# Attention output transposed by the DMA crossbar instead of TensorE and VectorE

## The chip, the cores and the metric

The kernel runs on one core of a Trainium2 chip. The metric is the device time of one execution in microseconds. Runs of one comparison share a chip and are taken in turn with the kernel before. A ratio is the mean time of one kernel's fast runs over the mean of the other's fast runs in the same rounds, so it is not quite the ratio of the medians quoted beside it. The experiments ran on several chips, each beside its own runs of the kernel before; the median of the kernel before moves from 243.7 to 244.9 us between these groups, so small differences between runs of different groups say nothing.

## The reference, cut to what matters

```python
B, H, S, D = 4, 8, 768, 64      # attention in chunks of 32, context 16 left, 8 right, 8 memory slots
out[:, :, c_start:c_end] = softmax(scale * q_c @ k_full.T) @ v_full      # for each chunk
x = attn_out.transpose(0, 2, 1, 3).reshape(B * S, H * D)                 # 3072 x 512
h = x @ w_in                                                             # 512 -> 2048
g = h + sin(alpha * h) ** 2 / (alpha + 1e-9)
return g @ w_out                                                         # 2048 -> 512
```

The first MLP matmul needs x with its 512 columns on the partitions. The attention gives it with the rows on the partitions, so each block of 96 rows has to be transposed.

## The kernel before

The kernel takes one batch after the other. While the attention of batch i+1 runs (a "burst"), the second MLP matmul of batch i is fed between its pieces, one matmul (`o`) at a time from a `Stream`. One block of a burst:

```python
def pv(b, j, pt):
    x_blk = blk.tile([QW, H, D], BF, name="x_blk")        # blk: 3 buffers
    ...
    for h in range(H):
        nc.tensor.matmul(otv[:, h // 4, h % 4, :], pt[...], vws[b % 2][:, h, j, 0:D + 1])
    nc.vector.reciprocal(rv, ...)
    nc.vector.tensor_tensor(out=x_blk..., in0=otv..., in1=rv..., op=ALU.mult)
    return x_blk, ot

def xt(xT, j, x_blk, ot):            # one block later
    ...
    for kt in range(KT):
        nc.tensor.transpose(xtp[:, kt, :], x_blk[:, 2 * kt:2 * kt + 2, :]..., ident[0:QW, 0:QW])
    nc.vector.tensor_copy(xT[:, :, QW * j:QW * j + QW], xtp)

def burst(b, stream, shares, lag):
    ...
        ptl[s] = qk_exp(s)                       # scores (sc) and exp
        stream.take(n // 3, True)
        xbl[s - lag] = pv(b, s - lag, ptl.pop(s - lag))
        stream.take((n + 1) // 3, True)
        xt(xT, s - lag - 1, *xbl.pop(s - lag - 1))
        stream.take((n + 2) // 3, True)
```

After the burst comes an MLP stage: 16 groups of the first MLP matmul (`hT`), of which each reads all of xT. The q, k and v of the batch after next are loaded by GpSimd's queue, issued around the start of a burst (`load_qk(i + 2)`, `load_v_all(i + 2)`). The output stores are issued by SyncE.

The softmax here doesn't subtract the row's maximum and nothing guards it: scores larger than these inputs give would overflow.

## Time and profile before

| | kernel before |
|---|---|
| time, median of three runs | 243.7 us |
| TensorE busy, clock | 91% of the span, 0.986 |
| burst 1, 2, 3 (first sc to last x_blk) | 16.9, 19.8, 20.0 us |
| end of the burst (last x_blk to the fifth matmul of the first hT group) | 2.8, 2.8, 2.5 us |

The busy shares tell which engine is fullest over the span, but a change in one stage has to be read from that stage. So the table has bursts and their ends, taken from start and end times in the timeline. The fifth matmul of the first hT group is where the second half of xT is needed in the new order, and is a fair mark in both.

### The profile page before, as it was taken

How to read it: one execution, taken by the hardware profiler on the slowest of the kernel's cores; microseconds unless marked ns; L12 is line 12 of the kernel's file. 1: busy time of each engine (PE TensorE's matmuls, PEld its weight loads, DVE VectorE, ACT ScalarE, POOL GpSimd, SP SyncE). 2: the span in 40 equal slices, each digit the busy share in tenths (PEclk: the TensorE clock that was granted, in tenths of full speed). 3: DMA queues.
4: the chain of work that ended last, by engine and by line, in shares of the span. 5: the costliest groups of instructions: out<-in, count | busy, mean ns of one | idle time of the engine just before them, and what ended most of it. 6: DMA issues, size and time to landing. Idle time of an engine off the chain costs nothing.

```text
span 243.4 us, 4498 instructions
## 1 busy us (share of the span) xinstructions
PE 222.6 (91%) x1785; PEld 123.0 (51%) x1785; DVE 160.2 (66%) x287; ACT 154.7 (64%) x237; POOL 73.3 (30%) x96
## 2 busy tenths in 40 slices
PE   6798899989989899898999997998999999899994
PEld 2355565545445455454455653554455555453453
DVE  3496969999268658969457775868657267876101
ACT  3489599973975467798464784678765675871000
POOL 8899865214712114157200222120000002020000
PEclk9799999999999999999999997999999999999999
DMA  6999999999999610109992101001111101101122
GB/s 75 165 130 83 161 194 204 207 198 134 190 208 134 74 46 0 44 4 181 154 151 66 46 0 43 0 3 43 46 43 47 43 0 46 43 0 40 46 89 86
DMA packets 53852, 21.11 MB, mean 87 GB/s; under 512 B 36296, under 2 KB 50888, under 8 KB 53832
## 3 DMA queue, kind: packets, MB, share of 16 engines
q0 software_dynamic: 47616, 14.40, 70.7%
q1 hardware_dynamic: 6216, 6.43, 8.9%
q8 instruction: 14, 0.23, 0.4%
q14 instruction: 6, 0.05, 0.1%
HBM read 28.91 MB, written 6.29 MB: 145 GB/s over the span
## 4 chain that ended last, share of the span: by engine, by line
PE 48%; DVE 20%; ACT 12%; issue 12%; POOL 3%; DMA 2%; POOLq 1%; DVEq 0%; ACTq 0%
PE o L393 26%; PE hT L341 10%; DVE gT L367 8%; DVE s L358 5%; ACT pt L275 4%; ACT u L353 4%; ACT s L356 3%; PE ot L288 3%; PE sc L266 3%; POOL s L358 2%; DMA q_bf<-in_q_dram 2%; DVE kTi L243 2%; PE ot L306 2%; PE o L382 1%; DVE x_blk L293 1%
## 5 line engine op out<-in xcount | busy, mean ns | idle before, releaser
L393 PE MATMUL o<-w_out_sb,gT 128*128 128x512 bf16 x368 | 99.0, 381 | 0.7 <-DVE gT L367 0.4
L341 PE MATMUL hT<-xT,w_in_sb 128*128 128x384 bf16 x488 | 88.8, 329 | 3.9 <-DVE gT L367 3.6
L367 DVE SCALAR_TENSOR_TENSOR gT<-s,inv_alpha,hT 128x768 bf16<-128x768 f32 x61 | 61.2, 1012 | 30.0 <-ACT s L356 21.6
L353 ACT ACTIVATE u<-hT,alpha_sb 128x768 f32<-128x768 f32 x61 | 54.7, 898 | 28.3 <-PE hT L341 27.1
L341 PEld LDWEIGHTS <-w_in_sb 128*128 128x128 bf16 x512 | 49.8, 99 | 39.7 <-issue 7.4
L275 ACT ACTIVATE pt<-sc,biasm 128x256 bf16<-128x256 f32 x96 | 37.6, 492 | 13.0 <-PE sc L266 13.0
L393 PEld LDWEIGHTS <-gT 128*128 128x128 bf16 x368 | 31.9, 98 | 26.9 <-DVE gT L367 1.4
L358 POOL TENSOR_TENSOR s<-u 128x768 f32<-128x768 f32 x6 | 8.8, 1465 | 73.7 <-ACT u L353 73.7
L356 ACT ACTIVATE s<-u 128x768 f32<-128x768 f32 x34 | 28.7, 843 | 1.1
L358 DVE TENSOR_TENSOR s<-u 128x768 f32<-128x768 f32 x24 | 24.7, 1029 | 0.9 <-ACT u L353 0.8
L226 POOL COPY pr<-q_bf 128x768 bf16<-128x768 bf16 x12 | 10.1, 838 | 43.7 <-PE tt_a L242 27.4
L293 DVE TENSOR_TENSOR x_blk<-ot,rinv 96x512 bf16<-96x512 f32 x32 | 22.0, 686 | 1.1
L292 DVE RECIPROCAL rinv<-ot 96x8 f32<-96x8 f32 x32 | 6.4, 201 | 20.1 <-PE ot L288 19.8
L402 ACT COPY o_sb<-o 128x512 f32<-128x512 f32 x11 | 6.4, 585 | 20.0 <-PE o L393 20.0
L400 DVE COPY o_sb<-o 128x512 f32<-128x512 f32 x12 | 8.2, 687 | 15.4 <-PE o L393 15.4
L288 PEld LDWEIGHTS <-pt 128*128 128x128 bf16 x256 | 11.9, 97 | 7.2 <-issue 2.3
L171 PE MATMUL z<-zeros 128*128 128x512 bf16 x37 | 13.9, 463 | 1.3 <-DVE zeros L165 1.3
L288 PE MATMUL ot<-vw,pt 128*128 128x65 bf16 x256 | 13.0, 193 | 0.8 <-ACT pt L275 0.6
L266 PEld LDWEIGHTS <-kTi 64*128 64x128 bf16 x256 | 6.9, 94 | 13.0 <-issue 6.6
L266 PE MATMUL sc<-qT,kTi 64*128 64x96 bf16 x256 | 11.4, 205 | 1.8 <-ACT pt L275 1.2
L257 PEld LDWEIGHTS <-pr 128*128 128x128 bf16 x96 | 6.6, 100 | 12.5 <-issue 8.0
L306 PEld LDWEIGHTS <-x_blk 96*128 96x128 bf16 x128 | 8.4, 97 | 6.6 <-DVE x_blk L293 1.6
(66 smaller groups left out, 182.1 us busy)
## 6 DMA issues: line engine op xcount, KB each, us to landing
out_dram<-o_sb SPq DMA_DIRECT2D x23, 256.0 KB, 2.1
k_bf<-in_k_dram POOLq DMA_DIRECT2D x3, 768.0 KB, 8.6
q_bf<-in_q_dram POOLq DMA_DIRECT2D x3, 768.0 KB, 12.6
vw<-in_v_dram POOLq DMA_DIRECT2D x6, 384.0 KB, 17.4
w_in_sb<-in_moe_w_in_dram POOLq DMA_DIRECT2D x8, 256.0 KB, 8.3
w_out_sb<-in_moe_w_out_dram POOLq DMA_DIRECT2D x4, 512.0 KB, 18.7
k_bf<-in_k_dram POOLq DMA_DIRECT2D x4, 192.0 KB, 6.2
q_bf<-in_q_dram POOLq DMA_DIRECT2D x4, 192.0 KB, 6.7
```

Source lines behind the costliest of these rows:

```text
L171: nc.tensor.matmul(z[:], zeros[:, 0:P], zeros[:])
L266: nc.tensor.matmul(sc[:, e, QW * hp:QW * hp + QW], kTi[64 * e:64 * e + 64, hp, 104 * j:104 * j + P], qT[64 * e:64 * e + 64, hp, QW * j:QW ...
L275: nc.scalar.activation(pt[:, 0:H * QW].rearrange("p (g e c) -> p e g c", g=4, e=2)[:, :, :, 32 * m:32 * m + 32], sc[:, :, 0:4 * QW].rearra ...
L288: nc.tensor.matmul(otv[:, h // 4, h % 4, :], pt[:, QW * h:QW * h + P], vws[b % 2][:, h, j, 0:D + 1])
L293: nc.vector.tensor_tensor(out=x_blk[:].rearrange("p (g e) d -> p g e d", g=2), in0=otv[0:QW, :, :, 0:D], in1=rv.unsqueeze(3).to_broadcast( ...
L306: nc.tensor.transpose(xtp[:, kt, :], x_blk[:, 2 * kt:2 * kt + 2, :].rearrange("p e d -> p (e d)"), ident[0:QW, 0:QW])
L341: nc.tensor.matmul(hts[hf][:, 0:HALF], w_in_sb[:, kt, P * ft:P * ft + P], xT[:, kt, HALF * hf:HALF * hf + HALF], start=(kt == 0), stop=(kt ...
L353: nc.scalar.activation(u[:], hT[:, :, 0:HALF], ACTF.Sin, scale=alpha_sb[:, ft:ft + 1])
L356: nc.scalar.activation(s2[:], u[:], ACTF.Square)
L358: (nc.vector if sq == "D" else nc.gpsimd).tensor_tensor(out=s2[:], in0=u[:], in1=u[:], op=ALU.mult)
L367: nc.vector.scalar_tensor_tensor(out=gv, in0=s2[:], scalar=inv_alpha[:, ft:ft + 1], in1=hT[:, :, 0:HALF], op0=ALU.mult, op1=ALU.add)
L393: nc.tensor.matmul(o[:], gT[:, ft, P * s:P * s + P], w_out_sb[:, ft, :], start=(ft == 0), stop=(ft == FT - 1),)
```

## The change

The intent is to free TensorE, which is full in the bursts, of 96 transposes, and VectorE of 24 copies. `dma_start_transpose` is a transfer that writes a block transposed; it is issued by SyncE. "Landing" below is the moment at which the trace shows a transfer completed; the time to landing is counted from its issue. Batch 0 keeps the old way. Some o matmuls are moved behind the last block to cover the latency of the last transpose, and the first hT group reads the first half of xT's columns first.

```diff
-    blk = ctx.enter_context(tc.tile_pool(name="blk", bufs=3))
+    blk = ctx.enter_context(tc.tile_pool(name="blk", bufs=4))
@@ xt
-        if ot is None:
-            xtp = smp.tile([P, KT, QW], BF, name="xtp", tag="sm")[:]
-        else:
-            xtp = ot[:].bitcast(BF)[:, 0, 640:640 + KT * QW].rearrange("p (k c) -> p k c", k=KT)
+        if ot is not None:
+            nc.sync.dma_start_transpose(
+                xT[:, :, QW * j:QW * j + QW], x_blk[:].rearrange("p h d -> p (h d)"))
+            return
+        xtp = smp.tile([P, KT, QW], BF, name="xtp", tag="sm")[:]
@@ burst
-                xbl[s - lag] = pv(b, s - lag, ptl.pop(s - lag))
...
+                x_blk, ot = pv(b, s - lag, ptl.pop(s - lag))
+                if b > 0:
+                    xt(xT, s - lag, x_blk, ot)
+                else:
+                    xbl[s - lag] = x_blk
@@ l1
+        order = [(kt, hf) for kt in range(KT) for hf in range(2)]
+        if ft == 0:
+            order.sort(key=lambda o: o[1])
@@ main loop
-                xT = burst(i + 1, stream, (3, 3, 3, 4, 4, 4, 4, 4, 4, 4, 5, 5), 3)
+                xT = burst(i + 1, stream, (3, 3, 3, 4, 4, 4, 4, 4, 4, 4, 5), 3)
-                xT = burst(i + 1, stream, (16, 8, 6, 6, 6, 5, 5, 5, 5, 5), 1)
+                xT = burst(i + 1, stream, (16, 8, 5, 5, 5, 5, 5, 5, 3), 1)
-            stream.take(3)
+            stream.take(8 if i == 0 else 12)
```

More of the change, by code (lines that the diff above doesn't have):

```diff
@@ L322, in burst @@
             if 0 <= s - lag < NJ:
-                xbl[s - lag] = pv(b, s - lag, ptl.pop(s - lag))
-                if b == 0:
-                    xbl[s - lag] = (xbl[s - lag][0], None)
+                x_blk, ot = pv(b, s - lag, ptl.pop(s - lag))
[3 more added lines that the diff above has]
+                    xbl[s - lag] = x_blk
             stream.take((n + 1) // 3, True)
-            if 0 <= s - lag - 1 < NJ:
-                xt(xT, s - lag - 1, *xbl.pop(s - lag - 1))
+            if s - lag - 1 in xbl:
+                xt(xT, s - lag - 1, xbl.pop(s - lag - 1), None)
             stream.take((n + 2) // 3, True)
@@ L338, in l1 @@
             hts = [hT[:, 0], hT[:, 1]]
-        for kt in range(KT):
-            for hf in range(2):
-                nc.tensor.matmul(
-                    hts[hf][:, 0:HALF],
-                    w_in_sb[:, kt, P * ft:P * ft + P],
-                    xT[:, kt, HALF * hf:HALF * hf + HALF],
-                    start=(kt == 0), stop=(kt == KT - 1),
-                )
+        order = [(kt, hf) for kt in range(KT) for hf in range(2)]
+        if ft == 0:
+            order.sort(key=lambda o: o[1])
+        for kt, hf in order:
+            nc.tensor.matmul(
+                hts[hf][:, 0:HALF],
+                w_in_sb[:, kt, P * ft:P * ft + P],
+                xT[:, kt, HALF * hf:HALF * hf + HALF],
+                start=(kt == 0), stop=(kt == KT - 1),
+            )
         u = mlp.tile([P, 2, HALF], F32, name="u")
```

## The prediction

> **What bounds the kernel now.** I read the page first (busy shares, then the clock row), then the table of windows by stage, then the timeline of one stage, then the transfers. The page says that TensorE is the fullest engine at nearly full clock (0.986 over the span).
>
> ```profile
> PE 222.6 (91%) x1785; PEld 123.0 (51%) x1785; DVE 160.2 (66%) x287; ACT 154.7 (64%) x237; POOL 73.3 (30%) x96
> ...
> PEclk9799999999999999999999997999999999999999
> DMA  6999999999999610109992101001111101101122
> ```
>
> An average over the span does not say what bounds the stages that the change touches. Those are three "bursts": the attention of batches 1, 2 and 3, interleaved on TensorE with the second MLP matmul (o, line 393) of the batch before. I cut the span at their edges. Columns are length, then busy time and count of PE, PEld, DVE, ACT, POOL, then clock, DMA, GB/s.
>
> ```profile
> 58.00:80.00 22.00, 21.03 (x239) 11.35 (x240) 12.96 (x34) 14.44 (x30) 9.15 (x10) 1.00 2.60 169
> 80.00:113.00 33.00, 29.12 (x206) 17.37 (x205) 25.40 (x34) 24.17 (x30) 12.50 (x13) 1.00 0.24 43
> 113.00:134.00 21.00, 21.00 (x222) 10.87 (x221) 13.29 (x31) 12.49 (x28) 2.99 (x4) 1.00 1.81 133
> ...
> 166.00:190.00 24.00, 23.96 (x249) 12.64 (x249) 15.87 (x32) 15.66 (x32) 0.00 (x0) 1.00 0.12 45
> ```
>
> In the bursts (first, third and fourth line) PE is busy 96 to 100% and VectorE only 59 to 66%. So in a burst only TensorE's stream sets the time, and VectorE's 8 copies per burst (342 ns each, 2.7 us a burst) lie beside it. In the MLP stage between (second line) PE is at 88%: its gaps come from ScalarE and VectorE.
>
> Busy time overstates a pipelined matmul, so I take the price of one transposed block from the start times in the second burst's timeline (start, length, instructions):
>
> ```profile
> 121.57 0.41 PE L288 MATMUL ot<-vw,pt 128*128 128x65 bf16 x8
> 121.81 0.59 PE L393 MATMUL o<-w_out_sb,gT 128*128 128x512 bf16 x2
> 122.25 0.34 PE L306 MATMUL ot<-ident,x_blk 96*128 96x96 bf16 x4
> 122.42 0.60 PE L393 MATMUL o<-w_out_sb,gT 128*128 128x512 bf16 x2
> 122.95 0.34 PE L266 MATMUL sc<-qT,kTi 64*128 64x96 bf16 x8
> ```
>
> From start to start: four transposes push the stream by 122.42 - 122.25 = 0.17 us, though the line says 0.34; eight pv matmuls by 0.24; one o matmul by 0.44 / 2 = 0.22. The two o matmuls ahead of sc take 0.53, so about 0.1 us is lost on entering sc. That loss also occurs elsewhere without a transpose ahead of it, so I don't count it as gained.
>
> **What the Trainium skill says.** "TensorE: Matmul & The Clock Gate", Part 4: PE-mode transpose, gives about 275 ns per 128x128 transpose in one kernel's context and notes that a copy out of PSUM must follow. Here one 96-row transpose lasts 206 ns and four in a row cost the stream 0.17 us: in an interleaved stream the removed work is cheaper than that figure suggests. "DMA: Bandwidth & Descriptors", DMA Transpose (X-bar), asks for issue from SyncE or ScalarE, two-byte elements, an SBUF destination and partitions in multiples of 16; bf16 with 96 rows fits. No transfer of the kernel before is such a transpose, so its speed isn't shown. The same page, Anatomy of one DMA, gives a fixed cost of about 2.0 us, mostly the receipt of the write, and, in Issuing engines are not separate DMA queues, says that all transfers interleave on the same 16 engines. The trace agrees with the second: the output stores of 256 KB land in 5.6 us beside the loads of the first burst, in 2.2 in the second.
>
> ```profile
> out_dram<-o_sb SPq DMA_DIRECT2D x4, 256.0 KB, 5.6
> ...
> vw<-in_v_dram POOLq DMA_DIRECT2D x2, 384.0 KB, 16.8
> ...
> out_dram<-o_sb SPq DMA_DIRECT2D x4, 256.0 KB, 2.2
> ```
>
> **The change part by part.**
>
> *Removed from TensorE:* 24 blocks x 0.17 us = 4.1 us (96 transposes, 1.36 us a burst), all in stages where PE is full. This is the whole direct gain, 1.7% of the time.
>
> *Removed from VectorE:* 24 x 0.342 = 8.2 us, all beside a fuller engine. Worth about 0. PSUM tile ot also comes free earlier, after the normalising multiply; but there is next to no PE wait for such a buffer in the bursts (0.2 us of ot behind x_blk in the whole trace). Worth 0 to 0.2 us.
>
> *Added to SyncE and DMA:* 24 transposes of 96x512 bf16, 96 KB each. Estimate of the latency L from x_blk written to TensorE free to use it: plain stores here land in 1.7 us at 128 KB and 2.1 us at 256 KB, so a plain 96 KB transfer would take about 1.6 us. A crossbar transpose writes short pieces and has more to describe; I add 0.5 to 1.5 us and take L = 2.6 us on quiet queues. Beside the loads of the first burst, in the ratio of the stores (5.6 to 2.2) but with less data to wait for, I take 4.5 us. Throughput isn't the matter: a block comes every 1.5 to 1.9 us, and several can be in flight; the fourth x_blk buffer allows 4 blocks x 1.5 us = 6 us or more before VectorE must wait for a transpose to have read.
>
> *Moved:* the sum of o matmuls stays, but shares move behind the last pv to cover L, and the first MLP group does the columns of blocks 0 to 3 first. In burst 1, 2 + 2 + 8 = 12 o matmuls follow the last pv. In bursts 2 and 3 the code asks for 1 + 1 + 12, but a request stops at the end of a row block of 16: 57 have run before the 12, the block ends at 64, so only 7 run and 5 are carried into the MLP stage. That is 9.
>
> *The exposed wait at the end of each burst.* From the start of the last pv, x_blk is written 1.37 us later (pv at 130.96, multiply starts at 131.64 and lasts 0.69). The second half of the first MLP group then needs 1.37 + L. What TensorE has to do until then: pv 0.24, the o matmuls at 0.215, the key transposes of the next batch (0.28, absent at the end of burst 3), and the first half, 4 matmuls at 0.163 = 0.65.
> - Burst 1: cover 0.24 + 2.58 + 0.28 + 0.65 = 3.75; need 1.37 + 4.5 = 5.87; wait 2.1 us.
> - Burst 2: cover 0.24 + 1.94 + 0.28 + 0.65 = 3.11; need 3.97; wait 0.9 us.
> - Burst 3: cover 2.83; need 3.97; wait 1.1 us.
>
> Together 4.1 us, as much as is gained. The MLP stage after a burst gives some of it back: ScalarE and VectorE drain their work during the wait, and that stage has gaps of its own (33.0 - 29.1 = 3.9 us in the second line of the windows), of which I let the waits absorb a third, 1.3 us. Sum: -4.1 + 4.1 - 1.3 = -1.3 us, so 243.7 - 1.3 = 242.4 us.
>
> **The rivals.**
> - *The transposes are fully hidden.* If L is 1.5 to 2.0 us even under load, the waits shrink to 0 to 0.5 us each and the time is 243.7 - 4.1 + 0.5, about 240. For it: the shares and the order of the first group look tuned for just this. Against it: the fixed cost of plain stores is already near 1.4 us by extrapolation from 128 and 256 KB to nothing, and the first burst has loaded queues.
> - *The DMA wait takes the place of the gain and more.* If L is 4 us quiet and 7 under load, the waits are 4.6 + 2.3 + 2.5 = 9.4 us and the time is about 248 with some absorbed. In burst 1 a store of 256 KB goes into the same queue just ahead of the last transposes. For it: DMA is full in slices 2 to 13, where burst 1 lies. Against it: transposes have little data each. With such an L the x_blk buffers would bind too, so that VectorE, and through it PSUM and TensorE, would wait in the middle of burst 1.
> - *ScalarE becomes the bound of the bursts.* With a transpose less, a steady block takes about 1.5 us of TensorE in burst 1 and 1.7 in the others; exp needs 3 x 0.42 = 1.25 us. There remain 0.25 us or more, less the copies of o (0.59 us in every sixth block or so). It would hold back at most some 0.5 us of the gain.
>
> **Range and chances.** The gain is nearly fixed at 4.1 us; the uncertainty is three waits, each moving one to one with L. L lower by 0.6 everywhere gives about 240.5; L higher by 1.2 quiet and 2 loaded gives about 246. Faster by over 2% needs 4.9 us, more than all of TensorE's removed time: 6%. Slower by over 2% needs waits over 9 us: 8%. The rest is within 2%. Range 239.2 to 246.2.
>
> **What would show it right or wrong.** In the profile after: PE has 96 instructions fewer and the bursts, measured from the first sc to the last pv, are each shorter by 1.0 to 1.4 us; VectorE's busy time falls by about 8 us without any gain of its own; transposes show 2.2 to 3.2 us to landing outside the loads and about twice that in burst 1; hT of line 341 waits for a DMA into xT three times, 0.5 to 2.5 us each, longest after burst 1. It is wrong if there are no such waits (then 240), if VectorE waits for x_blk in mid-burst (then over 246), or if the bursts shrink by much less than 1 us, which would mean that TensorE's stream was not what set their length.

## The result, and the profile after

The kernel after takes 255.0 us (253.9 to 257.4, four fast runs) against 243.9 us (four runs of the kernel before, with one more than above). The ratio is 1.046, with a 95% interval of 1.036 to 1.055. It is slower, by 11 us, where 1.3 us of gain were predicted.

The page of the kernel after, busy shares and the rows of slices:

```profile
PE 217.3 (86%) x1665; PEld 118.5 (47%) x1689; DVE 152.0 (60%) x263; ACT 154.5 (61%) x237; POOL 74.3 (29%) x96
...
PEclk9999999999999579999999999999999799999999
DMA  7999999999999910018999400101143101100222
```

VectorE lost 8.2 us and TensorE has 96 weight loads fewer, as meant. TensorE's share fell from 91% to 86%, so it waits more, and its clock has dips to 0.5 and 0.7 in slices 14 and 15 and to 0.7 in slice 32. DMA is still full in slices 2 to 14.

Two groups of instructions, with the idle time just before them and what ended it, first in the page before, then in the page after:

```profile
L341 PE MATMUL hT<-xT,w_in_sb 128*128 128x384 bf16 x488 | 88.8, 329 | 3.9 <-DVE gT L367 3.6
...
L293 DVE TENSOR_TENSOR x_blk<-ot,rinv 96x512 bf16<-96x512 f32 x32 | 22.0, 686 | 1.1
```

```profile
L346 PE MATMUL hT<-xT,w_in_sb 128*128 128x384 bf16 x488 | 89.9, 331 | 18.0 <-DMA xT<-x_blk 13.9
...
L293 DVE TENSOR_TENSOR x_blk<-ot,rinv 96x512 bf16<-96x512 f32 x32 | 22.0, 687 | 12.8 <-DMA xT<-x_blk 12.0
```

TensorE now stands 13.9 us before hT, waiting for a transpose to land. VectorE stands 12.0 us before it may write an x_blk, because an earlier transpose hasn't read that buffer yet. Neither wait existed before.

The same windows cut as before (length, then busy time of PE, PEld, DVE, ACT, POOL, then clock, DMA, GB/s), one for burst 1 with its end, one for the MLP stage, one for burst 2 with its end, one for burst 3:

```profile
58.00:88.00 30.00, 20.34 (x208) 10.39 (x211) 11.58 (x28) 14.30 (x30) 10.06 (x11) 0.89 1.97 159
88.00:118.50 30.50, 28.33 (x180) 16.49 (x182) 22.09 (x29) 23.31 (x29) 10.61 (x10) 0.94 0.16 32
118.50:145.00 26.50, 20.76 (x204) 10.42 (x208) 13.95 (x27) 14.17 (x30) 5.39 (x7) 1.00 1.57 151
175.00:198.00 23.00, 20.44 (x198) 9.96 (x201) 11.38 (x22) 15.01 (x31) 0.00 (x0) 0.99 0.30 82
```

Burst 1 has nearly 10 us without TensorE and burst 2 nearly 6. Burst 3, where no load runs, has 2.6.

The timeline of the kernel after, around the end of burst 1 (start, length, engine and line, then idle time before and what ended it):

```profile
80.12 0.69 DVE L293 TENSOR_TENSOR x_blk<-ot,rinv 96x512 bf16<-96x512 f32 x1 [2.23 <-DMA xT<-x_blk]
...
80.16 0.81 PE L346 MATMUL hT<-xT,w_in_sb 128*128 128x384 bf16 x4 [2.29 <-DMA xT<-x_blk]
...
80.83 1.24 SPq L302 DMA_TRANSPOSE xT<-x_blk  x1
...
87.36 1.44 PE L346 MATMUL hT<-xT,w_in_sb 128*128 128x384 bf16 x4 [6.39 <-DMA xT<-x_blk]
...
88.84 0.90 ACT L358 ACTIVATE u<-hT,alpha_sb 128x768 f32<-128x768 f32 x1 [13.04 <-PE hT L346]
```

The last x_blk of burst 1 is itself 2.2 us late for want of a buffer. Its transpose goes out at 80.83, and TensorE can go on at 87.36, 6.5 us later.

The transposes of the kernel after by window, with the median from issue to landing: those issued up to 79 us, the first three of burst 2, the last five of burst 2, and burst 3:

```profile
xT<-x_blk SPq DMA_TRANSPOSE x7, 8.7
...
xT<-x_blk SPq DMA_TRANSPOSE x3, 9.2
...
xT<-x_blk SPq DMA_TRANSPOSE x5, 2.3
...
xT<-x_blk SPq DMA_TRANSPOSE x8, 3.2
```

The same instruction takes 2.3 us or over 9. The median of all is 7.5. A transfer whose landing the trace doesn't resolve is not in a median, so these rest on three, three, two and two transposes. The two behind the third line were issued at 140.3 and 141.6 us, after the last load had landed at 137.2. In burst 3, where no load runs, the two are 2.3 and 4.1 us; the slower one was issued 0.6 us after a store that itself took 4.3 us instead of the 2.0 to 2.2 of a store alone. In the run with DMA transposes in batch 3 alone the same pair took 2.3 and 2.4 us. So a smaller lateness without loads exists and stays open.

In burst 3 the removed work can be seen in the timeline (TensorE only):

```profile
182.25 0.41 PE L288 MATMUL ot<-vw,pt 128*128 128x65 bf16 x8
182.50 1.02 PE L398 MATMUL o<-w_out_sb,gT 128*128 128x512 bf16 x4
183.45 0.34 PE L266 MATMUL sc<-qT,kTi 64*128 64x96 bf16 x8
```

Between pv and sc there are now four o matmuls and nothing else, 0.95 us, where the kernel before had 0.17 us of transposes among them.

### The profile page after: what moved, and what is told of

It reads as the page before. It is cut to its first block, busy times and chain, and to the rows that moved or that the text cites. A ratio compares the mean times of both kernels' runs of the same rounds, so it can differ in the third digit from the quotient of the medians.

```text
span 252.1 us, 4332 instructions
## 1 busy us (share of the span) xinstructions
PE 217.3 (86%) x1665; PEld 118.5 (47%) x1689; DVE 152.0 (60%) x263; ACT 154.5 (61%) x237; POOL 74.3 (29%) x96
## 4 chain that ended last, share of the span: by engine, by line
PE 39%; DVE 18%; DMA 14%; issue 12%; ACT 10%; POOL 3%; SPq 1%; POOLq 1%; DVEq 0%; ACTq 0%
PE o L398 21%; DMA xT<-x_blk 11%; PE hT L346 10%; DVE gT L372 7%; DVE s L363 5%; ACT u L358 3%; DVE x_blk L293 3%; PE sc L266 3%; DMA q_bf<-in_q_dram 2%; POOL s L363 2%; ACT pt L275 2%; ACT s L361 2%; PE ot L288 2%; PE o L387 1%; DVE kTi L243 1%
## 5 line engine op out<-in xcount | busy, mean ns | idle before, releaser
L346 PE MATMUL hT<-xT,w_in_sb 128*128 128x384 bf16 x488 | 89.9, 331 | 18.0 <-DMA xT<-x_blk 13.9
L398 PE MATMUL o<-w_out_sb,gT 128*128 128x512 bf16 x345 | 91.2, 384 | 1.9 <-issue 0.7
L398 PEld LDWEIGHTS <-gT 128*128 128x128 bf16 x368 | 33.7, 99 | 33.0 <-issue 2.3
L275 ACT ACTIVATE pt<-sc,biasm 128x256 bf16<-128x256 f32 x96 | 37.4, 496 | 10.2 <-PE sc L266 10.1
L363 DVE TENSOR_TENSOR s<-u 128x768 f32<-128x768 f32 x24 | 24.1, 1004 | 4.2 <-ACT u L358 4.1
L226 POOL COPY pr<-q_bf 128x768 bf16<-128x768 bf16 x12 | 12.1, 1012 | 15.2 <-DMA q_bf<-in_q_dram 8.4
L171 PE MATMUL z<-zeros 128*128 128x512 bf16 x36 | 13.2, 451 | 1.4 <-DVE zeros L165 1.3
L266 PEld LDWEIGHTS <-kTi 64*128 64x128 bf16 x256 | 6.8, 94 | 14.2 <-issue 10.1
L226 POOL COPY pr<-k_bf 128x768 bf16<-128x768 bf16 x8 | 6.6, 826 | 19.3 <-PE tt_a L242 14.0
```

Source lines behind the costliest of these rows:

```text
L171: nc.tensor.matmul(z[:], zeros[:, 0:P], zeros[:])
L226: (eng or nc.gpsimd.tensor_copy)(pr[:].rearrange("p r e d -> p e r d"), src[:, 2 * hp:2 * hp + 2])
L266: nc.tensor.matmul(sc[:, e, QW * hp:QW * hp + QW], kTi[64 * e:64 * e + 64, hp, 104 * j:104 * j + P], qT[64 * e:64 * e + 64, hp, QW * j:QW ...
L275: nc.scalar.activation(pt[:, 0:H * QW].rearrange("p (g e c) -> p e g c", g=4, e=2)[:, :, :, 32 * m:32 * m + 32], sc[:, :, 0:4 * QW].rearra ...
L346: nc.tensor.matmul(hts[hf][:, 0:HALF], w_in_sb[:, kt, P * ft:P * ft + P], xT[:, kt, HALF * hf:HALF * hf + HALF], start=(kt == 0), stop=(kt ...
L363: (nc.vector if sq == "D" else nc.gpsimd).tensor_tensor(out=s2[:], in0=u[:], in1=u[:], op=ALU.mult)
```

## The experiments

Theory 1: the transposes are late because loads are on the same 16 DMA engines at that time. Rival 2: four x_blk buffers and SyncE, which is busy 1.2 us with each transpose, are too slow by themselves. Rival 3: the transposes stand behind the 256 KB stores in one queue. Rival 4: the new schedule is itself the cause. All results were correct except in the two runs without loads, which were meant to be wrong.

### No loads beside the bursts

```diff
-            if i + 2 < B:
+            if i + 2 < B and False:
                 kq_next = load_qk(i + 2)
...
-                load_v_all(i + 2)
```

The same edit was made in both kernels.

> The kernel before without the loads of q, k and v of batches 2 and 3 (wrong result on purpose: those batches reuse what is in the buffers). It is the partner of the same cut in the kernel after. Both theories expect it within 1.5% of the kernel before (240 to 244 us), because in the bursts TensorE was 96 to 100% busy beside the loads already.

> The kernel after without the same loads (wrong result on purpose). Theory 1, the loads on the same 16 DMA engines make the transposes late: outside loads a transpose lands in 2.3 to 4 us, so here all 24 do (median 7.5 us after); VectorE's wait for x_blk falls from 12.0 us to under 1, TensorE's wait for xT from 13.9 to 2 to 6, and the time comes within 1% of the other kernel without loads (239 to 245 us). Rival 2, four x_blk buffers and transposes that SyncE issues one at a time (1.2 us each, stores between) are too slow by themselves: VectorE still waits 8 us or more and this is still slower than its partner by 3% or more (248 us or more).

Measured: the kernel before without loads 245.3 us (ratio to before 1.003, 0.996 to 1.010; within the 1.5%, though above the 244 us given), the kernel after without loads 240.9 us (0.985, 0.978 to 0.992). All transposes of the latter, in its list of issues (10 of the 24 are resolved; the longest took 3.7 us, beside a store in burst 3), the only wait of TensorE for xT, in its table of waits (total, times, longest), and VectorE's wait, in its page:

```profile
xT<-x_blk SPq DMA_TRANSPOSE x24, 2.3
```

```profile
PE hT L346 <- DMA xT<-x_blk: 4.1, 3, 1.7
```

```profile
L293 DVE TENSOR_TENSOR x_blk<-ot,rinv 96x512 bf16<-96x512 f32 x32 | 22.0, 686 | 1.5 <-DMA xT<-x_blk 0.4
```

The median fell from 7.5 to 2.3 us and VectorE's wait for x_blk fell from 12.0 to 0.4. Nothing but the loads was taken out, so it is the loads that make the transposes late, and rival 2 doesn't hold on its own: the same four buffers and the same SyncE are fast enough. It also speaks against rival 3, since the stores still stand in the queue. By what the loads act, the shared DMA engines or something else that loads use, this run doesn't separate; that part of theory 1 is argued. The change even gains here: 240.9 is 1.8% below its partner, where I had expected 1% at most. The schedule alone, below, is 1.2% faster than the kernel before, so most of this probably comes from it; it was not run without loads.

### Eight x_blk buffers

```diff
-    x_blk = blk.tile([QW, H, D], BF, name="x_blk")
+    x_blk = xbp.tile([QW, H, D], BF, name="x_blk")       # xbp: 8 buffers
```

> The kernel after with 8 x_blk buffers in place of 4, so that VectorE never waits for a transpose to have read. Theory 1: VectorE's 12.0 us of waits vanish and the last transposes are issued 3 to 6 us earlier, but they stand in the same loaded queue; the wait of TensorE at the end of burst 1 (2.3 + 6.4 us) shrinks by half at most; time 248 to 252 us. Rival 2, the buffers are the cause: TensorE's wait for xT falls below 5 us in all and the time is 245 us or less.

Measured: 251.7 us (ratio 1.031, 1.023 to 1.039), as theory 1 had it. VectorE no longer waits, and burst 1 itself shrinks from 20.3 to 16.0 us. But its end grows from 6.6 to 10.5 us, where I had expected its wait to shrink. From the table of waits:

```profile
PE hT L347 <- DMA xT<-x_blk: 12.2, 5, 4.9
```

So the shortage of buffers is a consequence of the lateness. It costs 3.3 us of the 11; the rest of the wait moves to the end of the burst.

### Stores issued by ScalarE

```diff
-                nc.sync.dma_start(out[row:row + P, :], o_sb[:])
+                nc.scalar.dma_start(out[row:row + P, :], o_sb[:])
```

> The kernel after with the output stores issued by ScalarE, so that no 256 KB store stands in the transposes' own queue or in SyncE's program. Rival 3, the transposes are late because they stand behind stores in one queue: the transposes' median to landing falls from 7.5 us to under 5, and the time to 249 us or less. Theory 1 [...]: first transposes of bursts 1 and 2 land somewhat earlier, median over 6 us, time 251 to 256 us. ScalarE pays 23 issues of 0.3 us, 7 us, which lies beside other work for the most part.

Measured: 258.8 us (1.060, 1.051 to 1.069), and the median to landing rose from 7.5 to 8.3 us; the first transposes of burst 2 took 9.4 and 9.2 us, not less than before. Rival 3 falls. The time was higher than I expected of either theory; I didn't follow up what the issues on ScalarE cost.

### The schedule without the DMA transposes

The moved shares, the order of the first hT group and the fourth buffer stay. TensorE and VectorE transpose as in the kernel before.

```diff
-        if ot is not None:
-            nc.sync.dma_start_transpose(...)
-            return
+        (transposes into ot, and the copy one block later, as before)
```

> The kernel after with TensorE and VectorE transposing as in the kernel before, so that only the moved shares, the order of the first MLP group and the fourth buffer remain of the change. If these are neutral, and the DMA transposes alone cost the 11 us: 242 to 245 us, within 1% of before. Rival 4, the new schedule is itself a cause: over 247 us.

Measured: 241.5 us (0.988, 0.981 to 0.996), a little under the expected range and better than both kernels. So rival 4 falls too: the schedule gains 2.2 us, and with it in place the DMA transposes cost 13.5 us (241.5 to 255.0). The stages of the three profiled runs, in us:

| | before | schedule alone | after |
|---|---|---|---|
| burst 1, its end | 16.9, 2.8 | 16.9, 3.0 | 20.3, 6.6 |
| MLP stage of batch 1 | 31.2 | 30.9 | 31.5 |
| burst 2, its end | 19.8, 2.8 | 19.0, 2.7 | 21.9, 3.2 |
| MLP stage of batch 2 | 33.8 | 31.3 | 31.3 |
| burst 3, its end | 20.0, 2.5 | 19.2, 2.4 | 18.1, 3.7 |
| from there to the end | 52.0 | 53.3 | 55.0 |

The schedule's gain shows in burst 2 and 3 (0.8 each, from o matmuls moved out, which come back as 1.3 us at the end) and in the MLP stage of batch 2 (2.5 in these profiles; only 0.8 against the 32.2 us which this stage had in two other runs of the old schedule). Which of its three parts does it wasn't tried.

### One batch at a time

```diff
-                if b > 0:
+                if b == 1:      # b == 2, b == 3 in the others
                     xt(xT, s - lag, x_blk, "dma")
```

> The new schedule with DMA transposes in batch 1 only (loads of q, k and v of batch 2 beside them). Theory 1: nearly all of burst 1's loss in the kernel after stays, 3.4 us inside the burst and 3.8 at its end less what the schedule alone has: 248 to 250 us against 241.5. If the loss came from effects that add up over the bursts, less than 245.

> The new schedule with DMA transposes in batch 2 only (loads of q, k and v of batch 3 beside them, ending before the burst does). Theory 1: 3 us inside the burst and half a microsecond at its end: 244 to 246 us. With 241.5 for none and 240.9 for batch 3 alone, the three differences should add up to the 13.5 us between none and all within 2 us.

> The new schedule with DMA transposes in batch 3 only, where no load runs; loads as in the kernel before. Against 241.5 us with none: TensorE saves 8 x 0.17 = 1.4 us in burst 3 and waits about 2 us at its end, as the trace of the kernel after shows (2.1 us). So 0 to +1 us: 241.5 to 242.5 us. A gain of 1 us or more would mean that the wait is absorbed later.

Measured: batch 1 alone 252.0 us (1.031, 1.025 to 1.037), batch 2 alone 245.4 (1.003, 0.997 to 1.008), batch 3 alone 240.9 (0.990, 0.986 to 0.994). Against 241.5 with none, that is +10.5, +3.9 and -0.7 us. They add up to 13.7 where all together cost 13.5. Batch 1 went beyond my 250: its last wait in that profile was 8.1 us. Batch 3 came out below my 241.5, but these medians are of runs on different chips. By the ratios to the kernel before of the same rounds the differences to none are +10.5, +3.5 and +0.3 us, together 14.3 against 14.0. So the loss is where the loads are, and in time the quiet burst can't be told from no change. In the profile of batch 3 alone the burst goes from 19.2 to 18.1 us and its end from 2.4 to 2.7.

### Loads moved out of the bursts

First without a gate. A second q and k buffer was added; v of batch 2 and q, k of batch 3 were issued in program order in the MLP stage of batch 1, v of batch 3 in that of batch 2.

```diff
+            if 0 < i < B - 1 and ft == 2:
+                load_v_all(i + 1)
+            if i == 1 and ft == 6:
+                kq_late = load_qk(3)
```

> The kernel before with a second q and k buffer and the loads moved out of the bursts: v of batch 2 and q, k of batch 3 are issued in the MLP stage of batch 1, v of batch 3 in that of batch 2. Right result. Control for the next run: TensorE sets the bursts' length with or without loads, so 242 to 246 us, as without loads at all (245.3).

> The kernel after with the same moves of loads, right result. Theory 1 (loads beside the transposes are the cause): bursts 2 and 3 are as without loads (17.9 and 18.1 us from first sc to last x_blk), burst 1 has only q and k of batch 2 in its first half and its last transposes land in 2 to 4 us; time 239.5 to 243 us, which is 1 to 2% below the control. Rival 2 or 4: 247 us or more.

Measured: the control 243.7 us (0.999, 0.992 to 1.005), as expected; the kernel after with moved loads 251.6 us (1.031, 1.023 to 1.040), far off. The timeline of GpSimd and TensorE in the latter shows why:

```profile
77.16 1.33 POOL L139 DMA_DIRECT2D vw<-in_v_dram  x1
...
91.07 1.44 PE L346 MATMUL hT<-xT,w_in_sb 128*128 128x384 bf16 x4 [11.59 <-DMA xT<-x_blk]
```

GpSimd had nothing to wait for between, ran ahead of TensorE, and began to issue v of batch 2 at 77.2 us, before the end of burst 1. The last transpose went out at 80.1 and TensorE waited until 91.1. The transposes of this one burst fall in two groups, the two issued in 75 to 78 us, and the last two, of 78.2 and 80.1 us (the median of these rests on the first of them; the landing of the last isn't resolved):

```profile
xT<-x_blk SPq DMA_TRANSPOSE x2, 2.6
...
xT<-x_blk SPq DMA_TRANSPOSE x2, 7.4
```

So the miss speaks for theory 1 too: after q and k had landed (the last at 74.7 us) and before v had filled the queues, the same instruction in the same burst lands in 2.6 us; with v on the queues, in 7.4. The loads of v of batch 3 ran ahead too, to 120.8 us, and the first two transposes of burst 2, which began at 122.8, took 6.9 and 5.0 us.

The variant with six x_blk buffers and more cover:

```diff
-    x_blk = blk.tile(...)
+    x_blk = xbp.tile(...)                                 # xbp: 6 buffers
-            stream.take(8 if i == 0 else 12)
+            stream.take(8 if i == 0 else 12, True)        # does not stop at a row block's end
```

> The same with six x_blk buffers and a last request that does not stop at the end of a row block, so that 14 o matmuls rather than 9 follow the last pv of bursts 2 and 3 (1.1 us more cover). Theory 1: the waits for xT at the end of bursts 2 and 3 fall from 1 to 2 us to under 1 us each; 238 to 241.5 us, faster than both kernels. If the time is that of the run before within 0.3%, the o matmuls that were moved up were as useful where they stood.

Measured: six runs from 242.2 to 247.1 us, three of them counted slow; the fast ones' ratio is 0.997 (0.987 to 1.007), which is no gain. In the profile (of a run counted slow) TensorE's waits for xT after bursts 2 and 3 were 1.1 us together, as expected, but that after burst 1 was 7.5 us, and its end 10.1 us long: the same collision with v of batch 2 stays.

Then gated: the loads stand behind a multiply that GpSimd can only do in the second MLP group, after the last transpose of the burst.

```diff
-            sq = (... else "ADAAPDADADAPADAD")[ft]
+            sq = (... else "APAADDADADAPADAD")[ft]        # P: GpSimd squares
+            if 0 < i < B - 1 and ft == 1:                 # after l1(...)
+                load_v_all(i + 1)
+                if i == 1:
+                    kq_late = load_qk(3)
```

> Control: the run with all transposes on TensorE in the new schedule (241.5 us), with the loads of v of batch 2, q, k and v of batch 3 moved behind GpSimd's multiply of the second MLP group, so that GpSimd can't run ahead and issue them into a burst. Loads do not matter to TensorE's bursts: 240.5 to 242.5 us.

> The kernel after with the same gated loads, right result. The run before it with loads moved but not gated failed because GpSimd ran ahead and put v of batch 2 on the queues at about 78 us, just when the last transpose of burst 1 went out (wait 11.6 us). Theory 1 as it now stands (a transpose is late only when loads are on the queues when it is): all last transposes land in 2.3 to 3 us, TensorE's wait for xT is 3 to 6 us in all, and the time is within 1% of the control on either side: 239 to 244 us. If it stays at 248 or more, theory 1 is wrong or incomplete.

> Gated loads, DMA transposes for the first five blocks of batches 2 and 3 only, TensorE for the last three and for all of batch 1. The last DMA transpose is then issued some 5 us before the first MLP group needs it and lands in 2.3: no wait. TensorE saves 10 x 0.17 = 1.7 us against the control: 239 to 240.5 us, faster than the kernel before by about 1.5%.

Measured, fast runs: the control with all transposes on TensorE 245.0 to 247.9 us, the kernel after 244.9 to 247.7, the mixed one 243.6 to 246.1 (ratios to before 1.012, 1.012 and 1.006). All three missed their times: the control was expected at 241.5. Against each other the fast runs are as expected: with the loads gated, all transposes by DMA cost nothing against TensorE, and the mixed kernel (ten blocks by DMA) is 0.6% below it, within the intervals. But three of the six runs of the kernel after took 250.3 to 252.6 us. They are counted slow because they are over 1.5% above the fastest; whether the chip or the transposes did it, these runs don't tell, and the median of all six, 249.0, is above the 248 that I had named against theory 1. So the times of this pair support theory 1 only weakly. The inside supports it better: in the profile of the kernel after with the gate (a run counted slow) every resolved transpose landed in 2.3 to 2.8 us but one of 4.2, beside a store in burst 3, and TensorE's waits for xT, which had been 13.9 us, were within the 3 to 6 expected (first line). The loss of the gate itself has a likely cause in the same table (second line):

```profile
PE hT L346 <- DMA xT<-x_blk: 6.0, 3, 3.1
...
POOL pr L226 <- DMA k_bf<-in_k_dram: 10.0, 1, 10.0
```

q and k of batch 3 now queue behind v of batch 2 and are late for the next stage, where they are needed at once; that MLP stage took 36.0 us instead of 31.3. What the moved multiply costs by itself was not tried. Two of these kernels had a first execution of 562 and 768 us, in the profile of the first a matmul of 384 columns took 687 ns instead of 331; the kernel before had one of 1241 us on a later chip. The profiles of the control and the mixed run fell on them, so their inside is not read here.

### Dummy matmuls in the waits

```diff
             stream.take(8 if i == 0 else 12)
+            spin((28, 8, 5)[i])
```

> The kernel after with dummy matmuls (28, 8 and 5 of 128x512, about 0.22 us each) ahead of the first MLP group, inside the time in which TensorE waits for the last transposes. If the clock lowered after those waits (0.82 in the 15 us after burst 1, 0.80 in the 7 us after burst 3) costs time: 252 to 253.5 us, 1.5 to 3 us less than the kernel after (255.0), and no digit under 9 in the clock row. If the MLP stage absorbs the lower clock: 255 us again.

Measured: 254.3 us (1.041, 1.036 to 1.047). The clock row of its page:

```profile
PEclk9689999999999979999999999999999999999999
```

The dips after burst 1 and burst 3 are gone but for one digit of 7 (slice 15; the 6 and 8 stand in the first microseconds). From the end of burst 3 to the end of the program it takes 53.3 us instead of 55.0, as the schedule alone does (and as the kernel after does without loads, where that dip is missing too), so there the lower clock had cost 1.7 us; the MLP stage after burst 1 took 31.5 us with and without, so there it cost nothing. This was short of the 1.5 us or more expected of a clock that matters, and in the whole time 0.7 us less can't be told from 0 with these intervals. The clock is at most a small part.

### Six blocks of batch 3

```diff
-                if b > 0:
+                if b == 3 and s - lag < 6:
```

> The new schedule with DMA transposes for the first six blocks of batch 3 only, the last two on TensorE. The sixth is issued some 5 us before it is needed and lands in 2.3 us: no wait at the end of burst 3. TensorE saves 6 x 0.17 = 1.0 us of 241.5: 240.2 to 240.8 us, equal to or a little better than all eight by DMA (240.9).

Measured: 241.3 us (0.987, 0.982 to 0.992), above the 240.8 expected at most. Its end of burst 3 is 2.4 us, without a wait, but the whole is not better than all eight blocks (0.990) or none (0.988) by more than the intervals. So the best versions found are the schedule without DMA transposes, or with them in batch 3: 240.9 to 241.5 us, about 1.1% below the kernel before. Between these three I can't choose.

## Why the prediction was wrong

**Direct gain, 24 x 0.17 = 4.1 us: right as a price.** Without loads the bursts are 1.5, 1.05 and 1.05 us shorter than with the same schedule on TensorE (15.4 against 16.9; 17.9 against 19.0; 18.1 against 19.2), 3.6 in all. In the old order only six of the eight blocks of a burst are transposed before its last pv, and 6 x 0.17 = 1.02; why burst 1 gained half a microsecond more isn't shown. Nothing was seen of a gain from VectorE's 8.2 us, as said, and nothing of the third rival, ScalarE as the bound.

**Latency beside the loads, "I take 4.5 us": this is the step that failed.** The three transposes of burst 1 that are resolved landed 7.7 to 8.8 us after issue, and after the last of them TensorE went on 6.5 us after x_blk was written. The first three of burst 2 took 7.3 to 9.6. Two errors lie in it. First, I scaled by the ratio of the stores, which would have made 2.6 x 5.6 / 2.2 = 6.6 us, and then took off two more because a transpose has "less data to wait for". Its data is not where the time goes. A transpose is 384 packets of 256 bytes against a store's 128 of 2 KB, and, as the packets' records show, it starts late:

```
                                   issued   first 256-byte packet   last of 384
after, burst 1, first transpose     65.82   69.97 (4.1 us later)    72.08
after, burst 2, first transpose    124.86  130.92 (6.1 us later)   132.32
after, burst 3, first transpose    181.55  182.72 (1.2 us later)   183.36
```

In all three a store was issued just ahead; its own packets began 3.5 and 4.6 us after its issue in bursts 1 and 2, and 0.8 us after it in burst 3. Without that store in the queue the transposes were no faster, so it isn't the store that holds them up. Until the store began, the records have packets of the loads on the engines and hardly anything else. What decides when the transposes' packets get their turn was not tried by itself. Second, I took burst 2 for quiet, from the stores' median of 2.2 us. That median rests on stores of 128.3 and 133.5 us, as the loads ended (the last landed at 129.8) and after. The one store that was issued in the middle of the loads, at 122.9 us in the kernel before, landed in 6.7 us, and I had not looked at it singly. At the end of burst 2, for which "need 3.97" was worked out, the queues were quiet again and the last transposes landed in 2.3; it is the first ones of this burst that were late.

**"The fourth x_blk buffer allows 6 us or more": right as a number, wrong as a comfort**, since the latency exceeded it. VectorE waited 12.0 us for buffers in mid-burst, and bursts 1 and 2 became 3.4 and about 3 us longer than with the schedule alone, where each should have become a microsecond shorter. This is my second rival, and I had put the chance of a loss at 8%; its mechanism, with its sign in the profile, is what happened, only with 7 to 10 us under load instead of 7, and without its 4 us on quiet queues.

**Latency on quiet queues, L = 2.6 us: near, but a term is missing.** From issue to landing it is 2.3. But L was defined from x_blk written to TensorE free, and without loads this is 3.9, 3.1 and 2.9 us at the ends of the three bursts. What I left out is SyncE: it spends 1.2 us on each transpose and 0.5 on a store between, so the last transpose was issued only 1.6, 0.7 and 0.4 us after its x_blk was written. (A slip on which nothing rests: 1.7 us at 128 KB and 2.1 at 256 KB extrapolate to 1.3, not 1.4.)

**The exposed waits, 4.1 us in all, one to one with L: the form was right, the size wrong.** TensorE waited 13.9 us before hT: 8.7 after burst 1, then 3.1 and 2.1, where 2.1, 0.9 and 1.1 were predicted; the longest was after burst 1, as said. Without loads it waited 1.7, 1.1 and 1.3, and that this too makes 4.1 is chance: with 2.6 us everywhere the prediction's sum gives 0.2, 0.9 and 1.1, which is 2.2. With 2.3 for the landing and the wait for SyncE added it gives 1.5, 1.2 and 1.3, close to each of the three.

**"I let the waits absorb a third": not seen.** The MLP stage after burst 1 took 31.5 us against 30.9 with no such wait before it, and 30.9 too without loads, after a wait of 1.7 us. That stage gave nothing back.

**What I left at nothing: the moved shares.** The schedule alone gained 2.2 us. Together, by the medians: -2.2 for the schedule, +10.5, +3.9 and -0.7 for the batches, +11.5 where 11.2 was measured.

## What to carry to other kernels

Before giving an engine's work to the DMA queues, look at what else is on these queues at the very time the result is needed, transfer by transfer and not by a median. A small transfer on a critical path can pay the latency of the loaded queues, not its own: here 2.3 us became 7 to 10. Count it from the data being ready, with the time that the issuing engine is still busy with the transfer before. And when loads are moved, look at when their engine can really issue them: an engine without a wait runs ahead of its place in the program.

## What the Trainium skill lacked or had wrong

- "DMA: Bandwidth & Descriptors", Anatomy of one DMA, gives about 2.0 us as the fixed cost of a transfer, in a section on transfers that GpSimd issues. Those of SyncE here fit it on quiet queues (1.7 us for a 128 KB store, 2.3 us for a 96 KB transpose). What the page lacks is the time of a small transfer beside other traffic: up to 9.6 us for the same transpose while loads are on the queues.
- The same page, Issuing engines are not separate DMA queues, is right in that moving the stores to ScalarE gained nothing (258.8 us). But it calls the time to initiate a transfer "usually small relative to the DMA itself". SyncE spent 1.2 us on each transpose of 2.3 us to landing, and 0.33 to 0.54 us on a plain store of 256 KB.
- "Advanced Engine Details and Errata", X-Bar Transpose (TRN2), says that "TRN2 transpose DMAs are as fast as regular DMAs". From issue to landing that wasn't so here: on quiet queues a transpose of 96 KB took 2.3 us, a plain store of 128 KB 1.7 and one of 256 KB 2.0 to 2.2. A plain transfer of the same block was not run.
- "TensorE: Matmul & The Clock Gate", Part 4: PE-mode transpose, gives a single transpose's duration and no start-to-start cost of transposes in a stream. Here four 96-row transposes of 206 ns each moved the next matmul by 0.17 us.
